# A gated mix of linear attention and a shift MLP: attention summed into w4's banks, and q's last columns computed turned

## The chip, the core and the metric

The kernel runs on one core of a Trainium2 chip. The metric is the device time of one execution in microseconds (us), as the median of several runs. The engines are PE (TensorE: matrix multiplications, with its weight loads shown as PEld), DVE (VectorE), ACT (ScalarE), POOL (GpSimd) and SP (SyncE, which here only issues DMAs). PE writes its results to PSUM, which has eight banks of 512 fp32 columns on 128 partitions; DVE and ACT read them out ("evict"), and DMAs move data between DRAM and SBUF or turn a tile inside SBUF by the crossbar.

## The reference

Inputs: x of 2048 tokens by 640 channels in bf16, attention weights wqkv (640 x 1920) and wo (640 x 640), MLP weights w1, w2 (640 x 640), w3 (640 x 1728), w4 (1728 x 640), and a gate vector. Only `A_x` is used as x.

```python
def _A_ref(x, wqkv, wo):
    H = 32; Dh = D // H                        # 32 heads of 20
    q, k, v = ...                              # x @ wqkv, by head
    phi = lambda t: jnp.where(t > 0, t + 1, jnp.exp(t)) + 1e-6
    pq, pk = phi(q), phi(k)
    kv = jnp.einsum("bhsd,bhse->bhde", pk, v)
    z = jnp.einsum("bhsd->bhd", pk)
    num = jnp.einsum("bhqd,bhde->bhqe", pq, kv)
    den = jnp.einsum("bhqd,bhd->bhq", pq, z)[..., None] + 1e-6
    return (num / den) @ wo                    # heads joined again
def _B_ref(x, w1, w2, w3, w4):
    h = _gelu(_layernorm(x) @ w1)
    hs = shifted(h) @ w2                       # four column groups, shifted by 1, -1, 2, -2 tokens
    x1 = x + hs
    return x1 + _gelu(_layernorm(x1) @ w3) @ w4
g = _sigmoid((x * gate_w).sum(-1, keepdims=True))
return g * _A_ref(...) + (1 - g) * _B_ref(...)
```

Attention is linear: the sum over tokens of phi(k) and v is a 20 x 20 matrix for each head, and the queries meet only that matrix (joined with wo into one 640 x 640 matrix M) and the sum z.

## The kernel before

The tokens are cut into 16 tiles of 128 (`t`) and four chunks of 512 (`c`); 640 channels are five blocks of 128 (`k`). "Turned" means channels on the partitions and tokens along the row; a plain tile has tokens on the partitions.

**Who sets the order.** Each engine has a queue that is worked through in order. The kernel's Python lists all pieces of work as named items in streams (`IT.add`, L330), with the items that must come before, a duration on PE and lags. A planner (`_Items.run`, L336) estimates when each item could start and takes the earliest; among equals, items with no PE work first, then the one with the longest chain of successors. Each chosen item emits its instructions at once to the queues of its engines. `_Sched` (L51) adds the waits: it knows which operation last wrote or read each piece of memory. PSUM is tracked by bank: an engine that wants a bank waits for the last operation of another engine on it.

**Banks.** `bank()` (L517) gives the free bank that is estimated to be free first, `pair()` (L534) two neighbours. `bank_hold` is the set of banks that can't be given out, because a sum in them is still open.

**Stages, as PE sees them.**
1. q and k (to 53.7 us): for each tile t a q tile (`q_tile`, L875) and a k tile (`k_tile`, L792), each five matmuls of 512 columns and five of 128 (130 for k, with two more columns for the sum of x and the gate's logit). Both end in `phi` (L783): an exponential on ACT into the ring `Er`, a `ts` on DVE and an `stt` on DVE that writes the plain tiles `pq_tok` (one row of tiles further on) or `pk_tok`. `gt_tail` (L809) follows with two matmuls. The gate (`gate_chunk`, L844) is taken four tiles at a time: a tanh on ACT and two small POOL operations put g into `stg[:, 2]` and 1 - g into `stg[:, 3]`.
2. The products of x and phi(k) (`gt_step`, L821) to 70.7, while DVE adds up z over 15 additions (`z_add`, L831). z is turned by the crossbar and spread to a full tile `zb`.
3. w1, w2 and the start of w3 (to 126): `w1_group`, `w2_tile`, `w3_group`, with layer norms on POOL and crossbar turns of the normalised tiles on SP (`t_xn`, L858). The loads of w3 (L1231) and w4 (L1234) are on SP's queue too. In this stage DVE also divides the queries: `qn_sum` (L1103) multiplies by `zb` and adds up by head, `qn_scale` (L1111) takes the reciprocal and scales; `qt_tile` (L1128) turns the result into `pqnT`.
4. w3, attention and w4 (126 to 256): `w3_group` (L1076) is five matmuls into a bank from `bank()` and a gelu on ACT into `h2T`, a ring of two chunks. `a_tile` (L1133) is the attention output of one tile: five matmuls of 512 columns and five of 128 into a pair; POOL has put (1 - g) x1 into `abx`, and a DVE `stt` (L1142) adds g times the pair to it, which frees the pair. `w4_half` (L1146) takes six banks for a chunk and writes w4's half block of 64 rows into them; for the first three chunks the last 128 columns are computed turned, in two tail banks (`w4_turned`, L1176), evicted by ACT into `mT` and turned back by the crossbar into `mtok`. `w4_tile` (L1195) adds the 13 full blocks for one tile and ends in a DVE `stt` for 512 columns and one for 128, which add (1 - g) times the sum to `abx`. The four attention tiles of chunk 0 lie between the last w3 groups of chunk 1; those of the next chunk come one after each w4 tile. Then come the 13 w3 groups of the chunk after that, and so on.

All four elementwise helpers have one line each for every use: `ts` L625, `tt` L633, `stt` L642, `activation` L659; five matmuls of `mm_group` are L603.

Of the kernel before, what the change touches and what calls it, by code (L numbers as in the profile page):

```python
# [5 lines left out]
BF16 = mybir.dt.bfloat16  # L6
F32 = mybir.dt.float32
ACTF = mybir.ActivationFunctionType
ALU = mybir.AluOpType

S = 2048
D = 640
# [404 lines left out]
def _build(nc, A_x, A_wqkv, A_wo, B_w1, B_w2, B_w3, B_w4, gate_w, out, dbg=None, stop=None):  # L417
# [47 lines left out]

    ones_c = pa.alloc("ones_c", [128, 768], BF16)
    ident = pa.alloc("ident", [128, 128], BF16)
    mask = pa.alloc("mask60", [128, 3, 20], BF16)
    mask_t = pa.alloc("mask_t", [128, 4, 3, 20], BF16)
    negh = pa.alloc("negh", [128, 4], F32)  # L470
# [20 lines left out]
    junk = pa.alloc("junk", [128, 1, D], BF16)  # L491
    qprod = pa.alloc("qprod", [128, D], F32)
    zacc = qprod
    zsum = pa.alloc("zsum", [128, D], BF16)
    xT = ra.alloc("xT", [128, KD, S], BF16)
    GT = ra.alias("GT", [128, KD, D], BF16, ra.last_addr, KD * S * 2)
# [9 lines left out]
    abx = rb.alloc("abx", [128, 4, D], F32)  # L506
    mT = rb.alloc("mT", [128, 2, 512], BF16)
    mtok = rb.alloc("mtok", [128, 2, 4, 128], BF16)
# [273 lines left out]

    def phi(b, dst, after_exp=None):  # L783
        se = slot("E", 3)
        src = psf[:, 512 * b:512 * b + D]
        activation(Er[:, se, :], src, ACTF.Exp)
        if after_exp is not None:
            after_exp()
        ts(dve, Er[:, se, :], Er[:, se, :], 1.0, EPS_PHI, ALU.min, ALU.add)
        return stt(dst, src, 1.0 + EPS_PHI, Er[:, se, :], ALU.add, ALU.max)  # L790

# [51 lines left out]

    def gate_chunk(c):  # L844
        cs = slice(4 * c, 4 * c + 4)
        activation(stg[:, 1, cs], lr[:, cs, 1:2].rearrange("p t o -> p (t o)"), ACTF.Tanh, scale=0.5)
        ts(pool, stg[:, 2, cs], stg[:, 1, cs], 0.5, 0.5, ALU.mult, ALU.add)
        ts(pool, stg[:, 3, cs], stg[:, 1, cs], -0.5, 0.5, ALU.mult, ALU.add)

# [13 lines left out]
    def warmup(cols, cyc):  # L863
# [9 lines left out]
        pe(fn, [], [ps[:, b, :]], cost=cols * cyc)  # L873

    def q_tile(t):  # L875
        tok = slice(128 * t, 128 * (t + 1))
        b = pair()
        mm_group(ps[:, b, 0:512], [(xT[:, k, tok], wq[:, k, 0:512]) for k in range(KD)])
        mm_group(ps[:, b + 1, 0:128], [(xT[:, k, tok], wq[:, k, 512:D]) for k in range(KD)])
        phi(b, pq_tok[:, t + 1, :])  # L880
# [45 lines left out]
    for i in range(3, NT + 2):  # L926
        if i < NT:
            addA(("q", i), 1.36, lambda t=i: q_tile(t))
            addA(("k", i), 1.36, lambda t=i: k_tile(t))
        if i > 3:  # L930
            for t in range(3) if i == 4 else (i - 2,):
                addA(("g0", t), 0.27, lambda t=t: gt_tail(t), deps=[(("k", max(t, 1)), 2.0)])
# [5 lines left out]
    def stats1(c):  # L938
        ln_chunk_stats(st1, c, lr[:, 4 * c:4 * c + 4, 0:1].rearrange("p t o -> p (t o)"))
        gate_chunk(c)  # L940

    for u in range(NT):
        if u % 4 == 0:
            IT.add("S1", ("s1", u // 4), 0.0, lambda u=u: stats1(u // 4), deps=[(("k", u + 3), 1.8)])
        d1 = [(("s1", u // 4), 3.0 + 0.9 * (u % 4))]
        d1.append((("k", 13), 0.0) if u == 0 else (("n1", u - 1), 0.9))
        if u >= 3:
            d1.append((("t1", u - 3), 0.0))
        IT.add("N1", ("n1", u), 0.0, lambda u=u: normalize(1, u, st1), deps=d1)
        IT.add("T1", ("t1", u), 0.0, lambda u=u: t_xn(1, u), deps=[(("n1", u), 1.1)] + ([(("zb",), 0.0)] if u == 12 else []))  # L950
    for u in range(1, NT):
        IT.add("Z", ("z", u), 0.0, lambda u=u: z_add(u), deps=[(("k", NT - 1), 2.0)] if u == 1 else [])
# [158 lines left out]
    def qn_scale(t):  # L1111
        sd = qn_slot[t]
        ts(dve, dnr[:, 0, sd, :], dnr[:, 0, sd, :], EPS_PHI, None, ALU.add, ALU.bypass)
        dve(lambda e: e.reciprocal(dnr[:, 1, sd, :], dnr[:, 0, sd, :]), [dnr[:, 0, sd, :]], [dnr[:, 1, sd, :]], cost=350.0)
# [18 lines left out]
    def a_tile(t):  # L1133
# [4 lines left out]
        tok = slice(128 * t, 128 * (t + 1))  # L1138
        b = pair()
        mm_group(ps[:, b, 0:512], [(pqnT[:, j, tok], M_sb[:, j, 0:512]) for j in range(KD)])  # L1140
        mm_group(ps[:, b + 1, 0:128], [(pqnT[:, j, tok], M_sb[:, j, 512:D]) for j in range(KD)])
        stt(abx[:, sa, :], psf[:, 512 * b:512 * b + D], stg[:, 2, t:t + 1], abx[:, sa, :], ALU.mult, ALU.add)  # L1142

    w4_banks = {}

    def w4_half(t):  # L1146
        sl = (t // 4) % 2
        tag_chk("h2T", sl, t // 4)
        b0, b2, bt = pair(), pair(), pair()
        tiles = [((b0, b2)[i // 2] + i % 2, bt + i % 2, 128 * (i // 2)) for i in range(4)]  # L1150
        for i in range(4):
            w4_banks[t + i] = tiles[i]
        bank_hold.update((b0, b0 + 1, b2, b2 + 1, bt, bt + 1))

        turned = t < NT - 4

        def fn(e):
            ins = None
            for pr in range(2):
                for par, tail in ((0, False), (1, False)) if turned else ((0, False), (1, False), (0, True), (1, True)):  # L1160
# [3 lines left out]
                    if tail:  # L1164
                        ins = e.matmul(ps[:, bs, q0:q0 + 128], l, w4[rows, KFF, 512:D], start=(pr == 0), stop=False,
                                       skip_group_check=True)
                    else:
                        ins = e.matmul(ps[:, bm, :], l, w4[rows, KFF, 0:512], start=True, stop=False)  # L1168
            if turned:
                for par in range(2):  # L1170
                    rows = slice(64 * par, 64 * par + 64)
                    ins = e.matmul(ps[:, bt + par, 0:256], w4[rows, KFF, 512:D], h2h[rows, t // 4, :], start=True, stop=False)  # L1172
            return ins
        pe(fn, [h2h[:, t // 4, :], w4[:, KFF, :]], [ps[:, b, :] for b in (b0, b0 + 1, b2, b2 + 1, bt, bt + 1)], cost=760.0)

    def w4_turned(t):  # L1176
        sl = (t // 4) % 2
        tag_chk("h2T", sl, t // 4)
        tag_set("mtok", sl, t // 4)
        bt = w4_banks[t][1]  # L1180
        for par in range(2):
            o = ps[:, bt + par, 0:256].rearrange("p (n q) -> p n q", q=128)
            prs = [(w4[:, k, 512:D], h2T[:, sl, k, :].rearrange("p (n h q) -> p n h q", h=2, q=128)[:, :, par, :]) for k in range(KFF)]

            def fn(e, o=o, prs=prs):
                ins = None
                for i, (l, r) in enumerate(prs):
                    ins = e.matmul(o, l, r, start=False, stop=(i == KFF - 1))  # L1188
                return ins
            pe(fn, [x_ for p_ in prs for x_ in p_], [o], cost=KFF * 109.2)  # L1190
            activation(mT[:, sl, :].rearrange("p (n h q) -> p n h q", h=2, q=128)[:, :, par, :], o, ACTF.Copy)
        bank_hold.difference_update((bt, bt + 1))
        sch.dma("sp", mtok[:, sl, :, :], mT[:, sl, :], "trm%d" % sl, transpose=True)

    def w4_tile(t):  # L1195
# [4 lines left out]
        a = t % 4  # L1200
        b1, b2, q0 = w4_banks.pop(t)

        def grp(o, n0, n1):
            prs = [(h2T[:, sl, k, 128 * a:128 * (a + 1)], w4[:, k, n0:n1]) for k in range(KFF)]

            def fn(e):
                ins = None
                for i, (l, r) in enumerate(prs):
                    ins = e.matmul(o, l, r, start=False, stop=(i == KFF - 1), skip_group_check=(n0 > 0))  # L1209
                return ins  # L1210
            pe(fn, [x_ for p_ in prs for x_ in p_], [o], cost=KFF * ((n1 - n0) * 0.4167 + 2.5))
        parts = [(ps[:, b1, 0:512], 0, 512)]
        if t >= NT - 4:
            parts.append((ps[:, b2, q0:q0 + 128], 512, D))
        for o, n0, n1 in parts:
            grp(o, n0, n1)
        bank_hold.discard(b1)
# [23 lines left out]
    for c in range(NCH):  # L1241
        for j in range(KD):
            deps = [(("t1", u), 0.9) for u in range(4 * c, 4 * c + 4)] if j == 0 else []
            if c == 0 and j == 0:
                deps.append((LAST_EXP, None))
                deps.append((("ga", KD - 1), None))
            if c == 1 and j == 0:
# [13 lines left out]
    for u in range(NT):  # L1261
# [6 lines left out]
        IT.add("T2", ("t2", u), 0.0, lambda u=u: t_xn(2, u), deps=[(("n2", u), 1.1)] + ([(("mt",), 0.0)] if u == 12 else []))  # L1268
    IT.add("MISC", ("w3load",), 0.0, w3_load, deps=[(("k", NT - 1), 0.0), (("t1", NT - 1), 0.0)])
    IT.add("MISC", ("w4load",), 0.0, w4_load, deps=[(("kvt", 1), 0.0), (("t1", NT - 1), 0.0), (("z", NT - 1), 1.5)])  # L1270
    for c in range(NCH):
# [20 lines left out]
    for t in range(NT):  # L1292
        deps = [(("zb",), 1.0), (("q", max(t, 2)), 2.0)]
        if t < 7:
# [11 lines left out]
    for t in range(NT):  # L1306
# [8 lines left out]
        if t % 4 == 0:  # L1315
            deps4.append((("w3", min(c + 1, NCH - 1), KFF - 1), 0.0))
            if t == 0:
                deps4 = [(("w4h", 0), 0.0)]
# [58 lines left out]
```

## Time and profile before

| what | value |
|---|---|
| median of four runs | 260.37 us (260.29 to 261.67) |
| the profiled execution's own time | 260.3 us |
| its span, first to last instruction | 259.1 us |
| granted PE clock | 1.0 throughout |
| crossbar turns: x, normalised tiles, queries, z, the product matrix, mtok | 13, 32, 16, 2, 1, 3 |
| DMA traffic | 25.86 MB, mean 100 GB/s |

The profile comes from one execution, so sums are made against its 260.3 us. The span leaves out 1.2 us around the instructions. The busy share in forty slices shows which engines share the stages with PE:

```profile
DVE  2587877899914999999993403996004410034333
ACT  1396777751356867685854141005510045300000
POOL 5003995869962108767913201222002110012001
```

Each digit is a slice of 6.5 us in tenths. DVE is nearly full from slice 13 to 20 (84 to 136 us), where it evicts w2 and divides the queries; ACT has its gelus there. From slice 22 on both are idle for half or more of the time.

### The profile page before, as it was taken

What the parts mean: (1) busy time and instruction counts of PE and PEld (TensorE: products, weight loads), DVE (VectorE), ACT (ScalarE), POOL (GpSimd) and SP (SyncE); (2) the same over time, 40 slices, a digit from 0 to 9 for tenths busy, and PEclk for the clock granted to TensorE, in tenths of its full rate; (3) what the DMA queues carried; (4) which work ended last, traced back from release to release, by engine and by line L of the source; (5) the groups of instructions that cost most, each with busy time, mean ns of one, the idle gap of its engine ahead of it and who ended that gap; (6) DMA issues with size and microseconds to landing.
All of it is one profiled execution on the core that took longest, in us unless ns stands there. A gap on an engine that the chain in (4) does not pass through costs nothing.

```text
span 259.1 us, 4134 instructions
## 1 busy us (share of the span) xinstructions
PE 255.6 (99%) x1600; PEld 131.2 (51%) x1600; DVE 151.4 (58%) x290; ACT 109.6 (42%) x223; POOL 94.1 (36%) x152
## 2 busy tenths in 40 slices
PE   8999999999999999999999999999999999999996
PEld 4555555554445455554444555444465444645453
DVE  2587877899914999999993403996004410034333
ACT  1396777751356867685854141005510045300000
POOL 5003995869962108767913201222002110012001
DMA  7655889581854798652735651115010020010211
GB/s 225 190 149 147 175 198 165 162 144 39 110 112 95 126 405 271 77 103 50 89 64 114 129 76 20 28 25 152 0 23 0 0 101 3 0 20 3 102 51 51
DMA packets 54307, 25.86 MB, mean 100 GB/s; under 512 B 45668, under 2 KB 52877, under 8 KB 54288
## 3 DMA queue, kind: packets, MB, share of 16 engines
q1 hardware_dynamic: 52112, 21.21, 37.1%
q0 software_dynamic: 1168, 3.28, 5.3%
q10 hardware_dynamic: 1008, 1.11, 1.2%
q8 instruction: 12, 0.20, 0.3%
q14 instruction: 7, 0.06, 0.1%
HBM read 12.04 MB, written 2.62 MB: 57 GB/s over the span
## 4 chain that ended last, share of the span: by engine, by line
PE 96%; DMA 2%; SPq 0%; DVE 0%; issue 0%
PE ps L603 61%; PE ps L1209 18%; PE ps L805 8%; PE ps L1188 3%; DMA x_tok<-in_A_x_dram 2%; PE ps L898 2%; PE ps L1096 1%; PE ps L1168 1%; SPq L285 0%; DVE x_tok L642 0%; PE ps L899 0%; PE ps L977 0%; PE ps L1006 0%; PE ps L614 0%; PE ps L1172 0%
## 5 line engine op out<-in xcount | busy, mean ns | idle before, releaser
L603 PE MATMUL ps<-xnT,w 128*128 128x512 bf16 x360 | 81.3, 379 | 0.0
L659 ACT ACTIVATE h2T<-ps 128x512 bf16<-128x512 f32 x52 | 30.5, 598 | 60.4 <-PE ps L603 60.3
L603 PEld LDWEIGHTS ps<-xnT,w 128*128 128x128 bf16 x360 | 34.3, 98 | 38.3 <-issue 0.3
L625 POOL TENSOR_SCALAR abx<-x_tok,stg 128x640 f32<-128x640 bf16 x16 | 14.9, 928 | 99.3 <-DVE x_tok L642 94.6
L1209 PE MATMUL ps<-w,h2T 128*128 128x512 bf16 (+1 forms) x260 | 50.1, 347 | 0.0
L642 DVE SCALAR_TENSOR_TENSOR x_tok<-ps,stg,abx 128x512 bf16<-128x512 f32 (+1 forms) x20 | 13.3, 670 | 62.0 <-PE ps L1209 62.0
L625 POOL TENSOR_SCALAR xn<-x_tok,st 128x640 bf16<-128x640 bf16 x32 | 35.4, 1114 | 18.0 <-DMA xnT<-xn 17.6
L1209 PEld LDWEIGHTS ps<-w,h2T 128*128 128x128 bf16 x260 | 22.9, 98 | 22.0 <-issue 0.3
L659 ACT ACTIVATE Er<-ps 128x640 bf16<-128x640 f32 x32 | 22.5, 709 | 15.6 <-PE ps L603 7.8
L658 ACT ACTIVATE junk<-x_tok 128x640 bf16<-128x640 bf16 x32 | 23.6, 739 | 3.4 <-DVE x_tok L640 2.8
L603 PE MATMUL ps<-M_sb,pqnT 128*128 128x512 bf16 (+1 forms) x160 | 24.3, 299 | 0.0
L659 ACT ACTIVATE hsT<-ps 128x512 bf16<-128x512 f32 (+1 forms) x32 | 19.0, 594 | 12.1 <-PE ps L603 11.6
L603 PE MATMUL ps<-w,hsT 128*128 128x512 bf16 (+1 forms) x160 | 23.7, 299 | 0.0
L642 DVE SCALAR_TENSOR_TENSOR abx<-ps,stg,abx 128x640 f32<-128x640 f32 x16 | 14.1, 884 | 15.8 <-PE ps L603 8.8
L603 PE MATMUL ps<-wkg,xT 128*128 128x130 bf16 (+1 forms) x140 | 21.4, 299 | 0.0
L603 PEld LDWEIGHTS ps<-M_sb,pqnT 128*128 128x128 bf16 x160 | 13.6, 98 | 13.0
L603 PE MATMUL ps<-wq,xT 128*128 128x512 bf16 (+1 forms) x130 | 19.8, 299 | 0.0
L603 PEld LDWEIGHTS ps<-w,hsT 128*128 128x128 bf16 x160 | 13.3, 98 | 12.3
L805 PE MATMUL ps<-pk_tok,x_tok 128*128 128x512 bf16 x80 | 17.8, 379 | 0.0
L625 DVE TENSOR_SCALAR Er<-Er 128x640 bf16<-128x640 bf16 x32 | 11.7, 367 | 8.0 <-ACT Er L659 7.6
L1125 DVE TENSOR_TENSOR pq_tok<-pq_tok,dnr 128x300 bf16<-128x300 bf16 (+1 forms) x48 | 15.7, 381 | 0.6
L640 DVE SCALAR_TENSOR_TENSOR x_tok<-ps,x_tok 128x640 bf16<-128x640 f32 x16 | 13.1, 820 | 4.4 <-PE ps L603 3.7
(84 smaller groups left out, 251.9 us busy)
## 6 DMA issues: line engine op xcount, KB each, us to landing
w<-in_B_w_dram SPq DMA_DIRECT2D x1, 2160.0 KB, 8.2
w<-in_B_w_dram SPq DMA_DIRECT2D x1, 2080.0 KB, 13.9
out_dram<-x_tok SPq DMA_DIRECT2D x3, 640.0 KB, 3.1
x_tok<-in_A_x_dram SPq DMA_DIRECT2D x2, 640.0 KB, 4.9
w<-in_B_w_dram POOLq DMA_DIRECT2D x8, 160.0 KB, 4.2
x_tok<-in_A_x_dram SPq DMA_DIRECT2D x5, 160.0 KB, 5.5
wv<-in_A_wqkv_dram POOLq DMA_DIRECT2D x1, 800.0 KB, 5.9
wq<-in_A_wqkv_dram ACTq DMA_DIRECT2D x4, 160.0 KB, 4.4
```

The source lines that it names most:

```text
L603: ins = e.matmul(out_ap, l, r, start=(i == 0), stop=(i == n - 1))
L625: return engf(lambda e: e.tensor_scalar(out_ap, in_ap, s1, s2, op0, op1), rd, [out_ap], cost=cost)
L640: return dve(lambda e: e.scalar_tensor_tensor(out_ap, in0, scalar, in1, op0, op1, accum_out=accum), rd, [out_ap, accum], cost=cost + 70.0)
L642: return dve(lambda e: e.scalar_tensor_tensor(out_ap, in0, scalar, in1, op0, op1), rd, [out_ap], cost=cost)
L658: return act(lambda e: e.activation(out_ap, in_ap, func, bias=bias, scale=scale, accum_out=accum), rd, wr, cost=cost)
L659: return act(lambda e: e.activation(out_ap, in_ap, func, bias=bias, scale=scale), rd, wr, cost=cost)
L805: ins = e.matmul(o, l, r, start=(t0 + q_ == 0), stop=(t0 + q_ == NT - 1))
L898: e.matmul(ps[:, b, 0:512], l, w[:, k, 0:512], start=(k == 0), stop=(k == KD - 1))
L1096: ins = e.matmul(o, l, r, start=st, stop=sp)
L1125: dve(lambda e, o=o, i0=i0, i1=i1: e.tensor_tensor(o, i0, i1, ALU.mult), [i0, dnr[:, 1, sd, :]], [o], cost=cost)
L1188: ins = e.matmul(o, l, r, start=False, stop=(i == KFF - 1))
L1209: ins = e.matmul(o, l, r, start=False, stop=(i == KFF - 1), skip_group_check=(n0 > 0))
```

## The change

1. *Gate.* The four tanh and eight POOL operations go. After the last k tile, one clip of all 16 logits to -60..60 on DVE (`gate_clip`), one exponential of the negated logits on ACT (`gate_exp`, before the first gelu), and three DVE operations after the last z addition (`gate_rest`): with e = exp(-logit), `stg[:, 2]` = e and `stg[:, 3]` = e / (1 + e) = 1 - g.
2. *Queries scaled by the gate.* `qn_scale` multiplies the denominator by e, so the queries carry a factor 1/e = g / (1 - g). One more multiplication by 1 - g, which w4's eviction makes anyway, gives g.
3. *Attention in w4's banks.* `a_tile` opens the sums that `w4_half`, `w4_turned` and `w4_tile` go on with: a held bank for each tile's 512 columns, and two tail banks for a chunk, opened with its last tile (first tile in chunk 3). For chunks 0 to 2 the tails are turned, ten matmuls of 256 columns for four tiles. `abx` gets no DVE operation any more. `w4_half` now needs all four attention tiles of its chunk.
4. *q's last columns turned.* For tiles 4 to 15 `q_tile` computes 512 columns only, in a single bank. For each of chunks 1 to 3, `q_turned` computes the last 128 channels for 512 tokens, `phi` writes them to `mT`, and `q_back` turns them into `pq_tok` by a crossbar DMA on SP. The third one stands ahead of the loads of w3 and w4.
5. *Memory.* `mT` moves so that it lives from the start, `mask_t` shares the place of `qprod`, and `ones_c` shrinks from 768 to 128 columns.

```diff
-    def phi(b, dst, after_exp=None):
+    def phi(b, dst, after_exp=None, n=D):
         se = slot("E", 3)
-        src = psf[:, 512 * b:512 * b + D]
-        activation(Er[:, se, :], src, ACTF.Exp)
+        src = psf[:, 512 * b:512 * b + n]
+        er = Er[:, se, 0:n]
+        activation(er, src, ACTF.Exp)
...
+    def gate_clip():
+        ts(dve, stg[:, 1, :], lr[:, :, 1:2].rearrange("p t o -> p (t o)"), LOGIT, -LOGIT, ALU.min, ALU.max)
+    def gate_exp():
+        activation(stg[:, 2, :], stg[:, 1, :], ACTF.Exp, scale=-1.0)
+    def gate_rest():
+        ts(dve, stg[:, 0, :], stg[:, 2, :], 1.0, None, ALU.add, ALU.bypass)
+        dve(lambda e: e.reciprocal(stg[:, 1, :], stg[:, 0, :]), [stg[:, 0, :]], [stg[:, 1, :]])
+        tt(dve, stg[:, 3, :], stg[:, 2, :], stg[:, 1, :], ALU.mult)
...
+    def q_turned(c):
+        b = bank()
+        sl = qx_slot[c] = slot("tl", 2)
+        mm_group(ps[:, b, :], [(wq[:, k, 512:D], xT[:, k, 512 * c:512 * (c + 1)]) for k in range(KD)])
+        phi(b, mT[:, sl, :], n=512)
+    def q_back(c):
+        sl = qx_slot[c]
+        sch.dma("sp", pq_tok[:, 4 * c + 1:4 * c + 5, 512:D], mT[:, sl, :], "trm%d" % sl, transpose=True)
     def q_tile(t):
         tok = slice(128 * t, 128 * (t + 1))
+        if t >= 4:
+            b = bank()
+            mm_group(ps[:, b, :], [(xT[:, k, tok], wq[:, k, 0:512]) for k in range(KD)])
+            phi(b, pq_tok[:, t + 1, 0:512], n=512)
+            return
...
+    IT.add("SG", ("sgc",), 0.0, gate_clip, deps=[(("k", NT - 1), 1.0)])
+    IT.add("SG", ("sg", 0), 0.0, gate_exp, deps=[(("sgc",), 0.2)])
+    IT.add("SG", ("sg", 1), 0.0, gate_rest, deps=[(("z", NT - 1), 0.0)])
...
     def qn_scale(t):
-        ts(dve, dnr[:, 0, sd, :], dnr[:, 0, sd, :], EPS_PHI, None, ALU.add, ALU.bypass)
+        ts(dve, dnr[:, 0, sd, :], dnr[:, 0, sd, :], EPS_PHI, stg[:, 2, t:t + 1], ALU.add, ALU.mult)
...
     def a_tile(t):
-        b = pair()
-        mm_group(ps[:, b, 0:512], [(pqnT[:, j, tok], M_sb[:, j, 0:512]) for j in range(KD)])
-        mm_group(ps[:, b + 1, 0:128], [(pqnT[:, j, tok], M_sb[:, j, 512:D]) for j in range(KD)])
-        stt(abx[:, sa, :], psf[:, 512 * b:512 * b + D], stg[:, 2, t:t + 1], abx[:, sa, :], ALU.mult, ALU.add)
+        i = t % 4
+        b = w4_banks[t] = bank()
+        bank_hold.add(b)
+        acc([(ps[:, b, :], [(pqnT[:, j, tok], M_sb[:, j, 0:512]) for j in range(KD)])], True)
+        if t >= NT - 4:
...
+        elif i == 3:
+            c = t // 4
+            for par in range(2):
+                bt = w4_tails[c, par] = bank()
+                bank_hold.add(bt)
+                acc([(ps[:, bt, 0:256].rearrange("p (n q) -> p n q", q=128),
+                      [(M_sb[:, j, 512:D], pqnT[:, j, 512 * c:512 * (c + 1)].rearrange("p (n h q) -> p n h q", h=2, q=128)[:, :, par, :])
+                       for j in range(KD)])], True)
...
     def w4_half(t):
-        b0, b2, bt = pair(), pair(), pair()
...
-                        ins = e.matmul(ps[:, bm, :], l, w4[rows, KFF, 0:512], start=True, stop=False)
+                        ins = e.matmul(ps[:, bm, :], l, w4[rows, KFF, 0:512], start=False, stop=False, skip_group_check=True)
...
     for t in range(NT):
-        deps = [(("zb",), 1.0), (("q", max(t, 2)), 2.0)]
+        deps = [(("zb",), 1.0), (("q", max(t, 2)), 2.0), (("sg", 1), 0.0)]
+        if t >= 4:
+            deps.append((("qb", t // 4), 3.0))
...
         if t % 4 == 0:
             deps4.append((("w3", min(c + 1, NCH - 1), KFF - 1), 0.0))
+            deps4.append((("a", t + 3), 0.0))
```

`acc` is a group of matmuls whose first and last flags are given by the caller, so that a sum can go on over several groups.

## The prediction

> **What bounds the kernel now.** I read the page first (busy times, slices, chain), then the chain in order of time, then the timeline of each stage.
>
> ```profile
> PE 255.6 (99%) x1600; PEld 131.2 (51%) x1600; DVE 151.4 (58%) x290; ACT 109.6 (42%) x223; POOL 94.1 (36%) x152
> PE 96%; DMA 2%; SPq 0%; DVE 0%; issue 0%
> ```
>
> TensorE (PE) holds 96% of the chain of waits. A busy PE could still be starved, so the chain in order of time has to show its pace:
>
> ```profile
> 50.98 2.72 PE ps L603 x20
> ...
> 70.70 4.32 PE ps L603 x20
> ...
> 153.96 2.94 PE ps L1188 x26
> ...
> 172.20 15.39 PE ps L603 x75
> ...
> 256.28 0.02 issue
> 256.31 1.08 DVE x_tok L642 x2
> ```
>
> The third row is four w1 groups of five 512-wide matmuls: 4.32/20 = 0.216 us each, 1.08 a group, and the trace grants clock 1.0. The row above is a q and a k tile (each five 512-wide and five of 128 or 130): 1.36 a tile, so 1.36 - 1.08 = 0.28 for five 128-wide, 0.056 each. With these two prices the stages can be added up. 172.20: one attention tile and 13 w3 groups, 1.36 + 13 x 1.08 = 15.40 against 15.39. 126.07 to 151.03: 18 groups and four attention tiles, 24.88 against 24.96. 94.16 to 125.40: 15 groups and 11 w2 tiles, 31.16 against 31.24. So PE runs at its own pace nearly everywhere from 13.4 to 256.3. About 0.1 us a stage is all that a freed engine could give back. Before 13.4 stands the load of x, behind 256.3 the last eviction (1.08) and store; the edit touches neither.
>
> **The change, part by part.**
>
> *q turned.* For 12 tiles the five 128-wide matmuls go: 12 x 0.28 = 3.36. Added: three groups of five 512-wide: 3 x 1.08 = 3.24. PE: -0.12.
>
> *Attention into w4's banks.* The 512-wide parts only change their bank. Tails of the last four tiles stay 128-wide. For the other twelve, 3.36 goes and 3 x 10 matmuls of 256 columns come. Price of one: the turned w4 row, 2.94/26 = 0.113 (this row holds its group's start too), or between the 512 and 128 prices, (0.216 + 2 x 0.056)/3 = 0.109. Sum 3.39 or 3.28: between +0.03 and -0.08. I take the middle, -0.03. w4's half step and its turned groups keep their matmuls; only a start flag goes.
>
> *Evictions.* 16 VectorE (DVE) operations leave:
>
> ```profile
> L642 DVE SCALAR_TENSOR_TENSOR abx<-ps,stg,abx 128x640 f32<-128x640 f32 x16 | 14.1, 884 | 15.8 <-PE ps L603 8.8
> L281 SPq DMA_TRANSPOSE mtok<-mT x3: 1189/1190/1407, 157.3 to 225.9; - x3
> ```
>
> 14.1 us less of DVE. That counts for nothing, since PE waited for DVE in none of the stages where they ran (139 to 254): the sums above leave no gap. On ScalarE (ACT) the q exponentials shrink by 12 x (709 - 598) ns and grow by 3 x 598: +0.46, less three of the four small gate operations (0.2 each). DVE in the q and k stage: 12 evictions go from 825 ns to somewhere between 750 (the 512-wide eviction of w4) and 660 (four fifths), and three come. Between 20.2 and 53.7 ACT is busy 24.3 of 33.5 and DVE 26.7, so both hide it. If that cover were gone, the three extra phi would cost at most 3 x (0.60 + 0.37 + 0.83) = 5.4.
>
> *Three crossbar turns on SyncE's queue (SP).* 3 x 1.19 us of issue, 2.4 to land (row above). Two fall in the q/k stage behind x's turns; the queue is otherwise idle there. The third stands ahead of the w3 and w4 loads. It waits for DVE's last q phi (about 56) but is placed behind the last normalised tile (near 87), so it waits for nothing, and the loads go out 1.2 later:
>
> ```profile
> 87.77 6.87 SPq L285 DMA_DIRECT2D w<-in_B_w_dram  x3
> 109.81 2.32 PE L603 MATMUL ps<-xnT,w 128*128 128x512 bf16 x10
> ```
>
> w3 is first used about 110.9 (second group of the lower row). Even with the longer landing on the page, 13.9, it is there by 87.8 + 1.2 + 13.9 = 102.9: 8 us of cover. The turned q columns are wanted first by the sums of tile 4, past 90.
>
> *Gate.* Four tanh become one clip, one exponential and three tiny DVE operations (each near the reciprocal's 0.35). The exponential is queued on ACT ahead of the gelu table load (68.98 to 70.26). Behind it wait all gelus of w1. The last k is evicted at 55.7, and the clip's successor chain is longer than the z additions', so the planner should put it ahead of them: done by 57, 12 us early. The rest of the gate, about 1.0 on DVE, sits between the last z addition (72.3) and the reduction at 77.59, which waited 5.3 for a DMA: free.
>
> *Banks.* This is the one new wait that could matter. After the fourth attention tile of a chunk, four main and two tail banks are held until w4 has used them. Two of eight remain for 3 + 13 + 13 w3 groups (end of chunk 1, chunks 2 and 3), where all eight were open. What queues behind a late bank is PE itself. Can two banks keep the pace?
>
> ```profile
> 173.40 14.19 PE L603 MATMUL ps<-xnT,w 128*128 128x512 bf16 x65
> 174.68 0.60 ACT L659 ACTIVATE h2T<-ps 128x512 bf16<-128x512 f32 x1 [17.35 <-PE ps L603]
> 175.75 0.60 ACT L659 ACTIVATE h2T<-ps 128x512 bf16<-128x512 f32 x1 [0.48 <-PE ps L603]
> ```
>
> A group that starts at 173.40 is read by ACT from 174.68 to 175.28. The same bank is wanted two groups on, 173.40 + 2.16 = 175.56. Slack 0.28, less the time L from ACT's end to PE's next weight load. No ACT to PE case stands alone in this trace; the nearest is DVE to PE at the start:
>
> ```profile
> 5.50 0.70 DVE L668 COPY xT<-ps 128x128 bf16<-128x128 bf16 x2 [0.43 <-PE ps L614]
> 6.25 0.10 PEld L898 LDWEIGHTS ps<-wq,xT 128*128 128x128 bf16 x1 [0.31 <-DVE xT L668]
> ```
>
> 6.20 to 6.25: L = 0.05. The far end is 0.42, the longest idle of the weight load that is put down to ACT (before w4's half step). I take 0.05, because it is a plain release of the same kind: cost 0 with 0.2 to spare, and ACT does nothing else in these stretches (0.48 idle before each gelu). At L = 0.42 a group takes (1.28 + 0.60 + 0.42)/2 = 1.15 in place of 1.08; some 25 groups (each run's first two find their banks free) x 0.07 = +1.8.
>
> *Order.* The tail tile 15 of attention moves ahead of w4's last half step: 1.36 moved, no more. w4's evictions, 0.75 + 0.34 on DVE every 4.2, free their banks long before the next attention tile needs one, since four others are open then.
>
> The Trainium skill, "TensorE: Matmul & The Clock Gate", Back-to-back issue gap, gives for a stream of loads and matmuls some 81 ns at 128 columns and 131 at 512. By it q alone would save 60 x 81 - 15 x 131 ns = 2.9 us; the rows above have 56 and 216, and they decide. Against the change speaks "Perfetto Trace Analysis", Optimization Strategy: a gap that repeats on the busy engine can mean that there isn't enough PSUM for the next tile. No row here has such gaps; by that rule the sum would be that of the two-bank case above.
>
> **Sum.** -0.12 - 0.03 = -0.15 us. Against the profiled execution's 260.3 (span 259.1 and 1.2 around it) that is 260.15; its time lies 0.07 below the median 260.37, so against the median 260.2.
>
> **The rivals.**
> 1. *Two banks are too few* (the other side): PE stalls at each w3 group of chunks 2 and 3. It decides from L above 0.28 us. For it: no row of ACT releasing PE, and any late gelu goes straight to PE. Against: 0.05 measured. Price +1.8, so 262.0.
> 2. *A new wait upstream.* The clip lands behind the z additions: exponential at 72.4, table load 1.3, first gelu 2 us late; ACT regains 0.48 a group over four groups, so the copy before the kv product (76.1) is nearly on time: 0 to +0.6. Or the loads' cover is gone: +1.2. Together 260.2 to 262.0, nearest 260.8.
> 3. *Wide matmuls give more* than their share, as the skill's rule has it, or a freed DVE lets the planner pack closer. The stage sums leave some 0.1 a stage over about twelve stages: at most -1.3, so 258.9 to 259.7. Against: the prices add up.
> 4. *It doesn't do what it says*: the planner lays q's turned groups where their exponentials delay k's. A k tile that ends at 23.77 has its banks back at 25.72, 1.95 later; the next use comes a k, a q and a tail later, 1.36 + 1.08 + 0.27 = 2.71. Two more exponentials of 0.6 in front would make it 0.4 late, three times: 261.4.
>
> **Chances.** Forecast 0.72, rival 1 0.13, rival 2 0.07, rival 3 0.05, rival 4 0.03. What can be told from no change is 0.5%, 1.3 us: 259.1 to 261.7. Rival 1 is slower, and half of 2 and 4; of rival 3 perhaps four fifths is faster. So faster 0.04, same 0.78, slower 0.18. The forecast's own range is 259.9 to 260.6 (the 256-wide price, the bounds on the gate and loads); reaching up to rivals 1 and 2, and down by part of rival 3, 259.6 to 262.0.
>
> **What would show it.** In the profile after: 20 matmuls of two tiles become 15 in 2.44 and the turned q group five in 1.08; no abx eviction on DVE; w3 of chunks 2 and 3 still 14.0 for 65 matmuls, with gelus 1.08 apart. If they stand 1.15 or more apart, or the chain goes through ACT h2T there, rival 1 holds. A table load later than 70.3 or idle PE before the kv product speaks for rival 2. I am wrong if the chain loses 1.3 us of PE time anywhere else.

## The result, and the profile after

The changed kernel takes 261.91 us (median of 46 executions, from 260.06 up) where the kernel before takes 260.19 (72 executions). The ratio is 1.0048, with a 95% interval of 1.0035 to 1.0060: a small loss, 1.25 us by this ratio, where the forecast was no change. Medians here are over all executions of a run, while ratios, intervals and counts leave out those with a granted clock below 1.0 or over 1.5% above the fastest; of the changed kernel's 46, 40 are left, with a median of 261.6.

The profiled execution hides the loss. It took 260.13 us, 0.17 less than the profiled execution of before, and the sum of the prediction was -0.15. The page of the changed kernel, busy time and the chain's shares by engine:

```profile
PE 255.9 (99%) x1525; PEld 129.4 (50%) x1525; DVE 143.5 (55%) x284; ACT 108.8 (42%) x223; POOL 92.3 (36%) x144
PE 99%; DVE 0%; issue 0%
```

Its chain in order of time (start, us, what):

```profile
20.55 2.44 PE ps L603 x15
...
25.98 3.52 PE ps L603 x20
...
70.37 4.32 PE ps L603 x20
...
173.35 14.03 PE ps L603 x65
...
207.60 14.03 PE ps L603 x65
```

The 20 matmuls of a q and a k tile have become 15 in 2.44 (2.72 before), and with a turned group they are 20 in 3.52, 1.08 more. w3 of chunks 2 and 3 holds 14.03 for 65 matmuls on two banks. ACT's timeline there (start, us, instruction, and in brackets the idle time ahead of it):

```profile
174.47 0.60 ACT L659 ACTIVATE h2T<-ps 128x512 bf16<-128x512 f32 x1 [17.32 <-PE ps L603]
175.54 0.60 ACT L659 ACTIVATE h2T<-ps 128x512 bf16<-128x512 f32 x1 [0.48 <-PE ps L603]
```

The gelus still stand 1.07 to 1.08 apart with 0.48 idle between them. The `abx` evictions are gone from DVE, as said. So this execution shows the terms of the sum, though its total comes so close by luck as well (see the point by point below). But 29 of those 40 executions of the changed kernel lie above 261 us, and of the kernel before 12 of 72. The question was what most executions lose that this one doesn't.

### The profile page after: what moved, and what is told of

It reads as the page before. It is cut to its first block, busy times and chain, and to the rows that moved or that the text cites. A ratio compares the mean times of both kernels' runs of the same rounds, so it can differ in the third digit from the quotient of the medians.

```text
span 258.8 us, 3990 instructions
## 1 busy us (share of the span) xinstructions
PE 255.9 (99%) x1525; PEld 129.4 (50%) x1525; DVE 143.5 (55%) x284; ACT 108.8 (42%) x223; POOL 92.3 (36%) x144
## 4 chain that ended last, share of the span: by engine, by line
PE 99%; DVE 0%; issue 0%
PE ps L603 53%; PE ps L1195 30%; PE ps L806 8%; PE ps L923 2%; PE ps L879 1%; PE ps L1127 1%; PE ps L1221 1%; PE ps L924 1%; PE ps L614 1%; DVE x_tok L642 0%; PE ps L1008 0%; PE ps L1037 0%; PE ps L1225 0%; PE ps L1218 0%
## 5 line engine op out<-in xcount | busy, mean ns | idle before, releaser
L603 PEld LDWEIGHTS ps<-xnT,w 128*128 128x128 bf16 x360 | 34.4, 98 | 39.3 <-issue 0.4
L625 POOL TENSOR_SCALAR xn<-x_tok,st 128x640 bf16<-128x640 bf16 x32 | 38.8, 1222 | 21.7 <-DMA xnT<-xn 21.2
L625 POOL TENSOR_SCALAR abx<-x_tok,stg 128x640 f32<-128x640 bf16 x16 | 13.3, 833 | 89.9 <-DVE x_tok L642 89.9
L659 ACT ACTIVATE Er<-ps 128x640 bf16<-128x640 f32 (+1 forms) x35 | 23.0, 663 | 15.6 <-PE ps L603 10.0
L1195 PE MATMUL ps<-M_sb,pqnT 128*128 128x512 bf16 (+1 forms) x100 | 21.0, 347 | 0.0
L603 PEld LDWEIGHTS ps<-wkg,xT 128*128 128x128 bf16 x140 | 11.9, 97 | 11.2
L633 DVE TENSOR_TENSOR qprod<-qprod,pk_tok 128x640 f32<-128x640 f32 x13 | 16.8, 1295 | 0.4
L1156 DVE TENSOR_TENSOR pq_tok<-pq_tok,dnr 128x300 bf16<-128x300 bf16 (+1 forms) x48 | 16.6, 399 | 0.6
L603 PE MATMUL ps<-wq,xT 128*128 128x512 bf16 (+1 forms) x70 | 16.4, 368 | 0.0
L625 DVE TENSOR_SCALAR Er<-Er 128x640 bf16<-128x640 bf16 (+1 forms) x35 | 12.3, 351 | 7.1 <-ACT Er L659 6.5
```

The costliest lines, as they stand in the source:

```text
L603: ins = e.matmul(out_ap, l, r, start=(i == 0), stop=(i == n - 1))
L625: return engf(lambda e: e.tensor_scalar(out_ap, in_ap, s1, s2, op0, op1), rd, [out_ap], cost=cost)
L633: return engf(lambda e: e.tensor_tensor(out_ap, a, b_, op), [a, b_], [out_ap], cost=cost)
L659: return act(lambda e: e.activation(out_ap, in_ap, func, bias=bias, scale=scale), rd, wr, cost=cost)
L1156: dve(lambda e, o=o, i0=i0, i1=i1: e.tensor_tensor(o, i0, i1, ALU.mult), [i0, dnr[:, 1, sd, :]], [o], cost=cost)
L1195: ins = e.matmul(o, l, r, start=first and i == 0, stop=last and i == len(prs) - 1, skip_group_check=True)
```

## The experiments

The theories, by the letters the expectations use: **A**, the third q turn pushes the loads of w3 and w4, the first turns of the second layer norm's tokens (`t2`; two of the expectations call them the turns of the gated tokens) queue behind them, and PE waits ahead of w3's first group. **B**, two banks are too few. **C**, PE waits in the q and k stage for turned tokens or a bank, because of order and contention there. **D**, the gate or the z chain. Later **M**, the change's memory edit moved nearly all buffers to addresses 32 off a multiple of 64, and **W**, of these w1's address alone costs. "Before" in each ratio is the kernel before on the same chip in the same session.

### First round: which part

**The changed kernel once more** (no edit).

> The changed kernel once more, for a profile of an execution that is slower than the first one (260.1 us). Theory A (loads): the third q turn sends the loads of w3 and w4 off about 1 us later against PE, the first normalised turns of the second layer norm land behind them, and PE stands before the first w3 group (near 109.6 us) for 1 to 3 us; all else keeps its pace. Theory B (two banks): PE loses 0.05 to 0.2 us at each w3 group of chunks 2 and 3, and their gelus are more than 1.08 us apart. Theory C (q and k stage): PE stands between 20 and 53 us, waiting for a turned x or a bank. Theory D (gate and z): PE stands between 70 and 90, behind z or the normalised tiles.

260.2 us, from a single execution. PE waited 0.2 for a turn ahead of w3's first group, and for no bank.

**The third q turn late:** behind the first four `t2` turns on SP, so that the loads of w3 and w4 go first (w4's load loses the same dependence).

```diff
-                       deps=[(("qx", i // 4), 2.5), (("t1", NT - 1), 0.0) if i == NT - 1 else (("k", i + 1), 0.0)])
+                       deps=[(("qx", i // 4), 2.5), (("t2", 3), 0.0) if i == NT - 1 else (("k", i + 1), 0.0)])
...
-    IT.add("MISC", ("w3load",), 0.0, w3_load, deps=[(("qb", NCH - 1), 0.0), (("k", NT - 1), 0.0), (("t1", NT - 1), 0.0)])
+    IT.add("MISC", ("w3load",), 0.0, w3_load, deps=[(("k", NT - 1), 0.0), (("t1", NT - 1), 0.0)])
```

> The third q turn is issued behind the first four normalised turns of the second layer norm in place of ahead of the loads of w3 and w4; nothing else differs on any queue. A: the stall goes, median 259.9 to 260.2, ratio to the kernel before 0.998 to 1.000. B, C and D: nothing changes, ratio 1.003 to 1.006.

260.69 us, ratio 1.0009 (0.9982 to 1.0035).

**Attention alone:** attention in w4's banks, the new gate and the memory moves; all q tiles as before, no turned q.

```diff
-        if t >= 4:
+        if False:
...
-            if i >= 4 and i % 4 == 3:
+            if False:
```

> Attention in w4's banks and the new gate alone, q as before (no turned q, no q turn on SP). A: no stall, ratio 0.999 to 1.001. B and D: the whole loss stays, 1.003 to 1.006. C: 0.999 to 1.001 like A.

262.18 us, ratio 1.0062 (1.0037 to 1.0088), the largest loss of all, without a single q turn. So A can't be the whole. Its profile loses time in the q and k stage: PE waited 1.6 us for `xT` and 0.8 for a bank there, and from w1 on it ran at its usual pace.

**w4's load late:** behind the first four `t2` turns.

```diff
-    IT.add("MISC", ("w4load",), 0.0, w4_load, deps=[(("qb", NCH - 1), 0.0), (("kvt", 1), 0.0), (("t1", NT - 1), 0.0), (("z", NT - 1), 1.5)])
+    IT.add("MISC", ("w4load",), 0.0, w4_load, deps=[(("t2", 3), 0.0), (("qb", NCH - 1), 0.0), (("kvt", 1), 0.0), (("t1", NT - 1), 0.0), (("z", NT - 1), 1.5)])
```

> The changed kernel with the load of w4 moved behind the first four normalised turns of the second layer norm on SP (the third q turn stays ahead of the load of w3). A: those turns no longer land behind 2 MB, the stall goes and the spread narrows, median 259.8 to 260.2, ratio 0.998 to 1.000. B, C, D: ratio 1.003 to 1.006.

260.15 us, ratio 1.0015 (0.9984 to 1.0046). The load lands in 8.8 us in place of 15.0. Both this kernel and the one with the late q turn came out lower than the changed kernel, yet they issue the same work up to 87 us. The changed kernel itself has one execution only in their session.

### Second and third round: addresses, or order

In the attention-alone kernel x's fourth load (chunk 3, 640 KB) landed after 8.5 us, in before after 5.6. The memory edit could do that, so it was tried by itself.

**Before, moved:** every buffer behind `ones_c` shifted by 288 bytes, to the changed kernel's addresses modulo 512. No instruction differs.

```diff
     ones_c = pa.alloc("ones_c", [128, 768], BF16)
+    pa.alloc("gap", [128, 144], BF16)
```

> The kernel before with one unused buffer of 288 bytes a partition put in behind ones_c, so that everything behind it (w3, w1, w2, wo_aug, x_tok, xnT, hsT ...) starts at the same address modulo 512 as in the changed kernel; no instruction differs. Theory M (where the tokens lie): the change's memory edit moved x_tok from an address that is a multiple of 64 to one that is 32 off, x's loads and turns take longer, and PE waits in the q and k stage; M expects the ratio of the change itself, 1.004 to 1.007, and x's fourth load at 6.5 us or more instead of 5.65. Theories C (order and contention: the same loads and turns are late because other work started earlier or later) and A (the third q turn pushes the loads of w3 and w4) expect no difference, 0.998 to 1.002.

261.53 us, ratio 1.0045 (1.0016 to 1.0074). It looked like M. The chain of this profile goes back through x:

```profile
29.15 7.49 DMA x_tok<-in_A_x_dram
36.65 6.24 DMA xT<-x_tok
42.94 2.90 PE ps L604 x20
```

x's fourth load takes 7.49, the first turn of chunk 3 then 6.24, and PE starts tile 12 only when it is there.

**The changed kernel, moved back** (224 bytes of gap), and **the same with w4's load late:**

> The changed kernel with one unused buffer of 224 bytes a partition behind ones_c, so that w3 to xn start at the same address modulo 512 as in the kernel before; no instruction differs. Theory M expects the loss gone: 0.998 to 1.001 against before (the working's sum of -0.15 us is 0.9994). Theories A and C expect 1.003 to 1.007 as without the gap.

> The changed kernel with the same gap and with w4's load put behind the first four turns of the gated tokens on SP. If M and A each own a part of the loss, this one is the fastest, 0.995 to 0.999 (259.0 to 260.0 us). If A owns it alone, it is where w4's load moved alone was, 1.0015 (0.998 to 1.005). If M alone, it equals the gap alone.

260.47 us, 1.0008 (0.9984 to 1.0031), and 260.09 us, 0.9992 (0.9970 to 1.0014).

**q alone:** the turned q groups and the memory moves on the kernel before, attention and gate as they were (the reverse of the attention-alone edit).

> The kernel before with q's last 128 columns of chunks 1 to 3 turned, the third turn ahead of w3's and w4's loads, and the memory moves; attention and the gate as before. M expects 1.003 to 1.006 (the address shift is in it); A expects the same, and PE waiting ahead of w3's first group around 109 us; C, if it is the attention and gate edit that sets the q and k stage's loads off, expects 0.998 to 1.001.

261.10 us, 1.0004 (0.9976 to 1.0031). Of the nine executions that count three lie above 261. So the whole loss doesn't come from q's turned columns and the memory moves alone. Its profile lost 1.8 us to the load of wq at the start.

**Before with `x_tok` alone moved**, a gap of 288 bytes ahead of it and 224 behind:

> The kernel before with x_tok alone moved by 288 bytes (a second unused buffer of 224 bytes behind it keeps xnT and all that follows at the same address modulo 512); no instruction differs. If it is the tokens' own address that costs (their loads write there, the turns read there), 1.003 to 1.007, as when all buffers moved (1.0045), with x's fourth load at 6.5 us or more. If the loss comes from another shifted buffer (w3, w1, w2, wo_aug, xnT, hsT), 0.998 to 1.002.

260.29 us, 1.0001 (0.9983 to 1.0018). The tokens' own address shows no cost.

**x's fourth load early**, in the changed kernel and in the kernel before: issued right behind the third, ahead of chunk 2's turns.

```diff
-    for c in range(1, NCH):
-        t0 = 5 if c == 1 else 4 * c
-        dma_in(x_tok[:, t0:4 * c + 4, :], x2[128 * t0:512 * (c + 1), :].rearrange("(n p) d -> p n d", p=128), "xc%d" % c)
+    for c in (1, 2, 3):
+        for l in ((1,), (2, 3), ())[c - 1]:
+            t0 = 5 if l == 1 else 4 * l
+            dma_in(x_tok[:, t0:4 * l + 4, :], x2[128 * t0:512 * (l + 1), :].rearrange("(n p) d -> p n d", p=128), "xc%d" % l)
         for t in range(4 * c, 4 * c + 4):
             x_turn(t)
```

> The changed kernel, addresses as they are, with x's fourth load issued right behind the third, ahead of chunk 2's four turns instead of behind them. If the loss is PE waiting for chunk 3's turned tokens (M and C agree on that), it goes: 0.996 to 1.001, and PE waits for no turned x between 20 and 53 us. If the loss lies in the loads of w3 and w4 (A) or is spread over every crossbar transfer, it stays at 1.003 to 1.006.

> The kernel before with the same reordering of x's fourth load and nothing else. Its own runs reach from 259.2 to 261.7 us; if that spread is the same wait met now and then, the median falls to 0.997 to 0.999 and the upper runs go; if the kernel before never waits there, 0.999 to 1.001.

The changed kernel: 260.62 us, 1.0010 (0.9991 to 1.0028); PE waits for no turn of x between 20 and 53 us. The kernel before: 259.70 us, 0.9988 (0.9972 to 1.0004).

**All three together** (gap, w4's load late, x's fourth load early):

> The changed kernel with the gap of 224 bytes, w4's load behind the first four turns of the gated tokens, and x's fourth load early. If the three losses add up, 0.995 to 0.998 (258.9 to 259.7 us) and a narrower spread than 259.3 to 261.5; if the early load only displaces chunk 2's turns, 0.999 to 1.003.

260.23 us, 0.9991 (0.9978 to 1.0004), from 259.39 to 260.65. The narrow spread came, the gain didn't: the upper executions went, the lower ones stayed.

### Fourth round: which address, or w1's time

**Before with w1 alone moved; before with all moved but w1 and `x_tok`; the changed kernel with w1 alone moved back** (gaps of 288 and 224 bytes around them):

> The kernel before with w1 alone moved by 288 bytes (224 more behind it keep w2 and all that follows at the same address modulo 512); no instruction differs. w1's eight pieces, rows of 256 and 64 bytes, are on the DMA engines beside x's fourth load. If w1's own address makes that load dearer and x's with it (theory W), 1.003 to 1.006; if not, 0.998 to 1.002.

> The kernel before with all buffers from w3 on moved by 288 bytes modulo 512 except w1 and x_tok, which stay where they were; no instruction differs. Theory W expects 0.998 to 1.002; if the loss is in w3, w2, wo_aug, xnT, hsT or what follows (turned tokens are written there), 1.003 to 1.007 as when all moved.

> The changed kernel with w1 alone back at its address of before modulo 512, all others as the change has them. Theory W expects the loss gone as with the gap for all, 0.998 to 1.002; without W, 1.003 to 1.007.

0.9979 (0.9957 to 1.0001), 0.9974 (0.9955 to 0.9993), 0.9990 (0.9967 to 1.0013). No part of the shift shows a cost, and w1's address doesn't either: W falls. The kernel before took 260.75 us beside these runs, where it took 260.05 to 260.38 beside the others, which lowers every ratio of this round. That kernels with the very instructions of before come out at 0.9974 also shows what a ratio of 12 executions can't tell.

**w1's and w2's loads late,** held until the ninth and tenth k tile:

```diff
-        dp = [k_done[5]]
+        dp = [k_done[8]]
...
-        dp = [k_done[8]]
+        dp = [k_done[9]]
...
-    IT.add("LW", ("lw1",), 0.0, load_w1, deps=[(("k", 5), 0.0)])
-    IT.add("LW", ("lw2",), 0.0, load_w2, deps=[(("k", 8), 0.0)])
+    IT.add("LW", ("lw1",), 0.0, load_w1, deps=[(("k", 8), 0.0)])
+    IT.add("LW", ("lw2",), 0.0, load_w2, deps=[(("k", 9), 0.0)])
```

> The changed kernel, addresses as they are, with w1's load held until the ninth k tile instead of the sixth and w2's until the tenth, so that neither is on the DMA engines with x's fourth load. If the loss is x's fourth load and its turns sharing the engines with w1's pieces, it goes: 0.997 to 1.001, and that load lands in under 6 us; if x's path is not where most executions lose, 1.003 to 1.006.

260.47 us where before took 260.75, ratio 0.9982 (0.9960 to 1.0004). x's fourth load lands in 4.9. The profiled span, 257.9, is the shortest of all twenty.

### Last round: the controls

> The changed kernel as it is, timed beside the kernel before on one chip, as the control for all runs above, of which every variant of the changed kernel came out at 0.998 to 1.0015. If the loss of 1.0048 belongs to the program, whatever the chip, 1.003 to 1.007. If it belongs to some chips or sessions, so that the variants showed nothing by being faster than 1.0048, 0.998 to 1.002.

> The kernel before with every buffer behind ones_c moved by 288 bytes, a second time (first 1.0045, 1.0016 to 1.0074). If the address of all buffers together costs, 1.003 to 1.007 again, though neither w1 alone (0.998), nor the tokens alone (1.0001), nor all others (0.9974) cost anything. If the first result was its session's, 0.998 to 1.002 and the address theory falls.

The changed kernel: 261.12 us, 1.0037 (1.0011 to 1.0063). The loss came back in another session. The moved kernel before: 260.35 us, 1.0001 (0.9983 to 1.0019), where it was 1.0045 the first time. M falls: its main support was one session's.

## Why the prediction was wrong

**A profile that shows the loss.** The repeat of the changed kernel was caught in a lossy execution, span 261.0 against 258.8. PE's waits (line, what it waited for: us in total, times, longest):

```profile
PE ps L614 <- DMA x_tok<-in_A_x_dram: 1.6, 1, 1.6
PE ps L603 <- DMA xT<-x_tok: 0.9, 1, 0.9
```

and its chain:

```profile
29.48 8.17 DMA x_tok<-in_A_x_dram
37.66 5.97 DMA xT<-x_tok
43.68 2.62 PE ps L603 x15
...
72.52 4.32 PE ps L603 x20
```

The w1 groups start at 72.52, not 70.37; what follows has its usual pace. Of the 2.15 lost, some 0.9 comes from the first loads of x (the first `gt_tail` row starts 0.87 later; PE waits for these loads in profiles of before too, 0.5 and 0.9 us). Another 0.9 is the wait at tile 12, whose turned tokens come too late. The remaining 0.35 lies between the two and was not traced to a cause. The kernel before has the wait at tile 12 in one profile only, that of its first run with all buffers moved (1.2).

**Where the cover went.** The cover of a transfer is the time from its landing to its first use. SP's and POOL's queues and tile 12's start on PE in before (timeline: start, us), and how long the first turn of chunk 3 took to land (DMA issues: count, us to landing):

```profile
26.04 7.11 POOL L285 DMA_DIRECT2D w<-in_B_w_dram  x8 [3.76 <-DVE pk_tok L642]
34.43 5.67 SPq L281 DMA_TRANSPOSE xT<-x_tok  x4
36.13 4.37 POOL L285 DMA_DIRECT2D w<-in_B_w_dram  x8
41.83 1.52 PE L603 MATMUL ps<-wq,xT 128*128 128x512 bf16 x10
```

```profile
xT<-x_tok SPq DMA_TRANSPOSE x1, 3.3
```

The same in the profile of the changed kernel:

```profile
25.26 7.26 POOL L285 DMA_DIRECT2D w<-in_B_w_dram  x8 [3.67 <-DVE pk_tok L642]
34.90 6.71 SPq L281 DMA_TRANSPOSE xT<-x_tok  x4
35.34 4.37 POOL L285 DMA_DIRECT2D w<-in_B_w_dram  x8
41.54 1.24 PE L603 MATMUL ps<-wq,xT 128*128 128x512 bf16 x5
```

```profile
xT<-x_tok SPq DMA_TRANSPOSE x1, 5.8
```

The first POOL row is w1's load, the other w2's. w1's is released by k tile 5 (the bracket: a `pk_tok` eviction). w2's, which needs k tile 8, has no bracket: it stands in POOL's queue behind w1's issue and the statistics of a layer norm, and follows w1's by 10.1 us in both. With narrower q tiles k tile 5 ends earlier: w1's load leaves 5.68 us after the first `gt_tail` row in place of 5.97, in all profiles that leave this load where it was, and that row itself follows one narrower q tile (0.27), so some 0.55 in all. The chain of x's loads and turns on SP isn't released by PE and doesn't move with it. In before the turn goes out after the last piece of w1's load has been issued and 1.70 us ahead of w2's load; now 0.44 ahead. It took 3.3, now 5.8. PE wants it at 41.83 and 41.54. The cover was 41.83 - 37.7 = 4.1 us; it is 41.54 - 40.7 = 0.8.

The same from all twenty profiles. Landing times and issues are from the DMA and timeline views, cover is tile 12's start on PE less the turn's landing:

| kernels | w2's load after the turn's issue, us | turn lands in, us | cover at tile 12, us |
|---|---|---|---|
| before; x_tok moved; w1 moved; rest moved; all moved (second) | 1.70, 1.09, 1.68, 1.74, 1.05 | 3.3, 2.6, 3.2, 3.3, 4.4 | 4.1, 4.2, 4.2, 4.2, 2.4 |
| changed; again; q late; w4 late; gap; gap and w4 late; w1 back | 0.44, -0.18, -0.18, -0.40, 0.25, 0.00, -0.08 | 5.8, 5.6, 5.0, 6.1, 5.4, 6.0, 5.6 | 0.8, 0.4, 1.2, 0.0, 1.0, 0.2, 0.7 |
| q alone | -0.13 | 5.2 | 0.7 |
| attention alone; all moved (first); changed, last repeat | -1.63, -0.77, -1.45 | 5.5, 6.2, 6.0 | none: PE waits 1.1, 1.2, 0.9 |
| w1 and w2 late | w1 1.02 | 3.4 | 4.7 |
| x's fourth load early (changed, before, all three) | 6.5, 6.6, 6.5, but 3.5 behind the start of w1's issue, which takes 7.3, 7.1, 7.3 | 6.7, 6.0, 6.1 | 6.1, 6.3, 6.7 |

A turn that is issued in a pause of POOL's loads and has 1 us or more ahead of the next one lands in 2.6 to 4.4 us (six profiles), one issued during such a load or less than 0.5 us ahead of it in 5.0 to 6.7 (fourteen). x's fourth load goes the same way against w1's: 4.9 to 5.7 us when it is issued well ahead of w1's, 5.4 to 8.5 behind it. The Trainium skill, "DMA: Bandwidth & Descriptors", Issuing engines are not separate DMA queues, has it that DMAs from different engines all run on the same DMA engines and interleave; the table agrees, and between its two groups of profiles a turn's landing differs by 2.4 us on average.

Three forms of the changed kernel have the cover back, w1 and w2 late (4.7 us), x's fourth load early (6.1) and all three edits together (6.7), and PE doesn't wait for the turn in their profiles; their ratios are 0.9982, 1.0010 and 0.9991 (intervals above). But the five forms that keep a short cover, 0.0 to 1.2 us, came out at 0.9990 to 1.0015 too. So the ratios don't show that giving the cover back is what removes the loss. The span less PE's waits for x, its turns and wq averages 258.5 over eleven profiles of the changed kernel and its forms (257.9 to 258.9) and 258.7 over seven of before (258.3 to 259.0): in line with the sum's -0.15, though the spread is larger than that.

**Point by point.**
- *Two banks* (rival 1, the likeliest besides the forecast): cost 0, as forecast; 14.03 for 65 matmuls in both stretches.
- *q turned, tails, evictions:* the two profiled executions differ by -0.17 against the sum's -0.15, but this closeness is partly luck. By the rows of PE's chain the span's -0.2 is made of four parts:

| stretch of PE's chain | before, us | changed, us | difference, us |
|---|---|---|---|
| start of the first full rows of q and k tiles | 13.43 | 13.21 | -0.22 |
| from there to the products of x and phi(k) (53.70, 53.37) | 40.27 | 40.16 | -0.11 |
| from there to w3's rows (126.07, 125.91) | 72.37 | 72.54 | +0.17 |
| from there to the last matmul's end (256.28, 256.05) | 130.21 | 130.14 | -0.07 |

  The second and the fourth are the edit's own terms, -0.11 of a forecast -0.12 and -0.07 within its bounds of +0.03 and -0.08. The first is x's first load, for which PE waited 0.5 in the one execution of before and not in the other. The third is a wait of PE that the next point explains.
- *Loads of w3 and w4:* "8 us of cover" was safe for w3's own landing (88.42 + 8.5 = 96.9), but overlooked that the turns of the second layer norm's tokens stand behind the loads. w4's load lands at 104.0 in place of 102.3, and the first of these turns now takes 4.3 us, not 2.6. The fourth tile's normalisation on POOL waits for that turn, and the fourth turn goes out at 106.90 in place of 104.94 and lands at 109.5. PE could have started w3's first group at 108.12 + 1.36 = 109.48; in before the turn landed at 109.1, 0.7 ahead of PE:

```profile
88.42 7.87 SPq L285 DMA_DIRECT2D w<-in_B_w_dram  x4
109.65 2.32 PE L603 MATMUL ps<-xnT,w 128*128 128x512 bf16 x10
```

  PE waited up to 0.2 for it in the profiles. A part of the loss in other executions may be here: not shown.
- *Gate:* hidden, as forecast, though the z additions grew (last section).
- *The step that failed* is in the first part: "Before 13.4 stands the load of x, behind 256.3 the last eviction (1.08) and store; the edit touches neither", with "the queue is otherwise idle there" for SP. PE ran at its own pace in the one profile, and I took that as proof that nothing fed it late. x is loaded until 34.4 and turned past 40, with 4.1 us of cover at tile 12, and I never priced that cover. Nor did I ask what an earlier k tile releases: two loads of 800 KB each on POOL's queue, straight onto that path. The runs show in its place a cover of 0.8 us, and none in the repeat, where PE waited 0.9. How much of the 1.25 us this step explains stays open. Rival 2 named a new wait upstream, but looked at the clip and at w3's and w4's loads.

**What stays open.** The late q turn, w4's late load, that one with the gap, and the two kernels with other addresses keep the short cover; still they came out at 0.9990 to 1.0015. Their intervals reach up to 1.0013 to 1.0046, those of the changed kernel down to 1.0011, so they may have met the wait as often and by chance less in their sessions; or w3's start owns a part; or the address shift matters only with other things; or the loss depends on the chip or session, since the changed kernel was not timed beside its variants, but for one execution.

The two halves of the edit speak against the narrower q tiles as the whole cause. The attention-alone kernel has the wide q tiles and w2's load at 36.03, as before, and lost most, 1.0062: its fourth load took 8.5 us, and what made that load slow wasn't found. q alone has the narrower tiles and a cover of 0.7 us, and its interval ends at 1.0031, below the changed kernel's 1.0035. The wait at tile 12 with a late turn stands in three profiles, but only one of them is of the changed kernel, and the other two have the wide q tiles. That a turn beside a POOL load lands later is shown; that the change makes this happen more often, and that it costs the 1.25 us, is argued.

## What to carry to other kernels

A busy engine at its own pace says that its feed is in time, not by how much: for each thing that the bounding engine consumes, subtract landing from first use, and treat a cover of a few us on a DMA path as a term that an edit can spend. When a piece of work becomes shorter, list what its end releases, loads on other queues above all, and ask which transfers they now meet. One profiled execution is a sample: where the spread between executions is as large as the effect, profile again until one of the slower ones is caught.

## What the runs showed of the hardware

A crossbar turn that is issued during a POOL load of eight pieces, or less than 0.5 us ahead of one, lands in 5.0 to 6.7 us (fourteen profiles); with a pause behind it and 1 us or more ahead of the next load it lands in 2.6 to 4.4 (six).

A shift of all buffers to addresses 32 off a multiple of 64 shows no cost that repeats: 1.0045 in one session, 1.0001 in the next, 0.9974 to 1.0001 for its parts. The Trainium skill, "DMA: Bandwidth & Descriptors", How a descriptor splits into AXI transactions, says that a descriptor which doesn't start at a multiple of 256 bytes costs extra beats; no run here shows it in the time.

DVE's fp32 z additions take longer now. The costliest groups of before and of the changed kernel, the z additions (busy us, mean ns of one):

```profile
L633 DVE TENSOR_TENSOR qprod<-qprod,pk_tok 128x640 f32<-128x640 f32 x13 | 14.1, 1081 | 0.4
```

```profile
L633 DVE TENSOR_TENSOR qprod<-qprod,pk_tok 128x640 f32<-128x640 f32 x13 | 16.8, 1295 | 0.4
```

The same instruction is a fifth slower. POOL starts the bulk of its normalising at 57.05 in place of 61.59, so the additions have 17.2 us of it beside them in place of 10.0. Three other kernels lie between: 1165 ns with 11.5 us (attention alone), 1209 with 15.0 (w1 and w2 late), 1254 with 16.4 (q alone). The gate's two small operations ahead of it, 0.9 us, are only a part of the earlier start: q alone still has them and starts at 59.16. It cost nothing here: the reduction that waits for z starts at 77.50, in before at 77.59.
